# Where the last p*v of each chunk stands, how far apart the score units are, and where the output weights are waited for

## The chip, the cores and the metric

The kernel runs on one core of one Trainium2 chip. The metric is device time in microseconds (us), from the start of the program to its end. The time before is a median of three executions, 561.78 us (561.67 to 562.17). One execution was profiled: 561.61 us, of which the span that the trace covers is 559.9 us.

The engines are named as in the profile: PE is TensorE (PEld its weight loads), DVE is VectorE, ACT is ScalarE, POOL is GpSimd, and SP is SyncE, which issues all DMAs here, in order, from one queue (SPq).

## What is computed

Two branches share the normalized input: windowed causal attention with 32 heads of 18, and a gated feed-forward layer. The result joins them.

```python
xn = layernorm(x)                                  # x is [1, 2048, 576], bfloat16
q, k, v = split(xn @ wqkv)                         # 32 heads, Dh = 18
scores = q @ k.T * Dh ** -0.5                      # a query sees itself and 255 keys before it
p = softmax(where(0 <= i - j < 256, scores, -1e9))
s = (p @ v) @ wo
h = sigmoid(xn @ w_gate) * (xn @ w_up)             # F = 4608
g = silu(h @ w_down)
out = x + s * g
```

## The kernel before

**Tiling.** The 2048 tokens go in four chunks of 512 (`CH`), a chunk in four blocks of 128 tokens. The contracted dimension of 576 is cut into 9 pieces of 64, so that most matmuls use half of PE's rows, and two of them run side by side in the two halves: the profile shows them as `64*128`. A chunk has these stages:

- Layernorm of four blocks, then transposes into `xn` (from chunk 1 on by eight DMA transposes, `xt`, line 250). `xn` is one buffer, so the transposes for the next chunk wait for the last gate/up step of this one.
- q, k and v projections, line 513, `64*128`, and DMA transposes of q and k into `qkp`.
- Gate/up, line 884, `64*128`: 324 *steps* of two matmuls with 512 columns each, 36 tiles of F in all. ACT takes the tanh of a tile, DVE multiplies it into `hT`.
- Attention is laid among the gate/up steps. A *score unit* (line 676, `64*128`) fills two PSUM banks for one group of four heads; ACT takes its exponent into a slot of `expr` (ring of `NEXP` = 10 slots), DVE masks it. A chunk has 8 head groups, with 4 units each in chunk 0 and 5 in the others. After two head groups comes their *p\*v* (line 733, `64*32`, eight small matmuls side by side): 72 matmuls in chunk 0 and 96 in the others. Four p\*v a chunk; `op_pv[c][NHG - 1]` is the fourth. A p\*v releases the `expr` slots of its units.
- After each p\*v a chain on DVE: transpose (line 749), reciprocal, multiplication, transpose back (line 766). Then SP issues copies from `op_` to `oT` (called `oc` in the code): eight behind the last p\*v.
- Output projection `wo` (line 802, `64*128`): two pairs of token blocks, 36 matmuls each.
- Down projection `f2` (line 1009, `128*128`): for each token block 9 steps of four pairs (512 and 64 columns). Chunk 0 runs blocks 0 and 1 step by step in turn, the others one block after the other. The last block of chunk 3 is line 1040.

So PE works with three forms of tile: `64*128` (projections, gate/up, scores, `wo`), `64*32` (p\*v) and `128*128` (down).

**What sets the order.** The program is not written in the order in which it runs. Every operation is an object with dependencies; `schedule()` is a list scheduler that places the operations of all engines on a modelled clock, and `emit()` writes each engine's instructions in that order. `deps` are dependencies that become semaphore waits (or PSUM and buffer hazards); `odeps` only hold the order in the planner and give no wait, since both ends are on PE, which runs in order. An operation of PE that depends on DMAs waits for one semaphore for each of their lanes; waits that the engine has already made are left out.

**What sets it around the change:**

- The k-th score unit of chunk c is not placed ahead of gate/up step `SC_AT[c] + k * SC_STEP[c]` (the list `gated`, in `build_ffn`). `SC_AT` is (108, 0, 0, 0). From chunk 1 on, the first unit is instead put behind the last down step of the chunk before.
- A p\*v of chunks 1 to 3 has an `avoid`: with `PV_AVOID` = (165, 280) and `PACKET` = 256 the planner puts a penalty of 20 us on starting it while the count of PE's instructions, modulo 256, lies from 165 to 280. p\*v has low numbers of columns, so its instructions go by fast.
- The first down step has an order dependency on the last gate/up step (`mms = [prev]`), and each later block on the last p\*v and (from block 2 on) on one `wo` pair.
- The projections of the next chunk run between down blocks 1 and 2. Their order is `QKV_NEXT`; v of block 1 comes behind the first `wo` pair and q of block 2 behind the second, if these have not been placed before.
- `wo` is loaded once, during chunk 0, by 12 DMAs on 12 lanes (`op_wo`, in `build_late_weights`), gated by gate tile 26. In `build`, the first `wo` pass of each pair of chunk 0 depends on all twelve. It also depends on the 16 lanes of the `oc` copies, as every chunk's first pass does.

Of the kernel before, what the change touches and what calls it, by code (L numbers as in the profile page):

```python
# [18 lines left out]
NHG = H // 4  # L19
# [31 lines left out]
SC_PRIO = 1  # L51
KD_PRIO = 0
SC_AT = (108, 0, 0, 0)
SC_STEP = (5.5, 5.0, 5.0, 5.0)
SC_PAD = 200.0
PV_PAD = 350.0
PACKET = 256
# [61 lines left out]
def mm_ns(n):  # L119
    return max(28.0, n / 2.4 + 2.5)  # L120
# [90 lines left out]
class Builder:  # L211
# [98 lines left out]
    def build(self):  # L310
        self.r_xr = Ring(NXR)
        self.r_xnr = Ring(NXNR)
        self.r_xn = Ring(1)
        self.r_w = Ring(RW)
        self.r_t = Ring(RT)
        self.r_pk = Ring(RPK)
        self.r_exp = Ring(NEXP)
        self.r_s = Ring(RS)
        self.r_xf = Ring(RXF)
        self.r_kd = Ring(RKD)  # L320
        self.r_rec = Ring(RREC)
        self.r_bn = Ring(RBN)
        self.op_f1 = {}
        self.build_init()
        self.op_pv = [[None] * NHG for _ in range(NCH)]
        self.op_sc = [[[] for _ in range(NHG)] for _ in range(NCH)]
        self.op_on = [[None] * NHG for _ in range(NCH)]
        self.op_mul = [[None] * NHG for _ in range(NCH)]
        self.all_kd = {}
        self.op_oc = [[[], []] for _ in range(NCH)]  # L330
        self.op_v = [None] * NQB
        self.op_tail = [None] * NHG
        self.op_hT = {}
        self.f2_last = None
        for c in range(NCH):
            self.build_ln(c)
            if c == 0:
                self.build_weights()
                self.build_wd()
            self.build_qkv(c)  # L340
            self.last_mul = None
            self.build_attn(c)
            self.load_x(c)
            self.op_pkz = [self.op("POOL", 2000, lambda e: e.memset(self.pk[:, 1:RPK, :, :], 0.0), f"pkz:{c}",
                                   deps=self.op_on[c], prio=1)]
            if c == 0:
                self.op_wo = []
            self.build_wo(c)
            self.build_ffn(c)
            if c == 0:  # L350
                self.build_late_weights()
                for o in self.ops:
                    if o.name in ("wo:0:00", "wo:0:10"):
                        o.add_dep(self.op_wo)

    def build_init(self):
        op = self.op
# [486 lines left out]
    def build_ffn(self, c):  # L844
# [27 lines left out]
        prev = None  # L872
        gated = [(SC_AT[c] + k * SC_STEP[c], u) for k, u in enumerate(u for l in self.op_sc[c] for u in l)]
        if c > 0:
# [40 lines left out]
        for n0, n1 in zip(cuts, cuts[1:]):  # L915
# [49 lines left out]
            o = self.pe((n1 - n0) * mm_ns(CH), f, f"f:{c}:{low[n0][1]}:{n0}", deps=deps, prio=3, psum=alloc, mode="r64")  # L965
# [19 lines left out]
            prev = o  # L985
            while gated and gated[0][0] <= n0:
                gated.pop(0)[1].odeps.append(o)
        for o in self.op_se:
            o.add_dep(prev)
        mms = [prev]  # L990
        self.r_xn.release(0, prev)
        f2_last = [None] * NWD
        self.f2_ops = f2_ops = {}
        prev = mms
        for blocks in (((0, 1), (2,), (3,)) if c == 0 else ((0,), (1,), (2,), (3,))):
# [5 lines left out]
            for q in range(NWD):  # L1001
                for i in blocks:
                    def f_f2(e, q=q, i=i, ps=banks[i]):
                        b = ps.banks[0] * 512
                        for fl in range(WDG):
                            ft = q * WDG + fl
                            lhsT = self.hT[:, ft, i * P:(i + 1) * P]
                            for n0, n1 in ((0, 512), (512, D)):
# [4 lines left out]
                    o = self.op("PE", WDG * (mm_ns(512) + mm_ns(64)), f_f2, f"f2:{c * QPC + i}:{q}", deps, 3,  # L1013
                                alloc=[banks[i]] if q == 0 else [], mode="full",
                                odeps=prev + ([self.op_wop[i - FIN]] if q == 0 and i >= FIN else [])
                                + ([self.op_pv[c][NHG - 1]] if q == 0 and i > 0 else []))
                    banks[i].users.append(o)
                    prev = [o]
# [326 lines left out]
```

## Time and profile before

| | before |
|---|---|
| median of three executions | 561.78 us |
| the profiled execution | 561.61 us |
| its span | 559.9 us |
| DVE busy | 317.7 us (57%) |
| ACT busy | 274.7 us (49%) |
| DMA share of 16 engines, queue q1 | 61.3% |
| granted TensorE clock in every slice | 1.00 |
| score units, chunk 1 | the first at 156.54 us, the last at 220.41 us |
| p\*v starts, chunk 0 | 59.20, 71.65, 84.53, 95.02 us |
| p\*v starts, chunk 1 | 174.07, 190.63, 206.97, 223.75 us |
| p\*v starts, chunk 2 | 310.70, 326.42, 342.76, 359.54 us |
| p\*v starts, chunk 3 | 448.55, 464.25, 486.42, 503.20 us |
| down starts (blocks 0 and 1), chunks 0 to 3 | 103.25, 245.77, 383.50, 516.93 us |

The last p\*v of a chunk stands 8 to 24 us ahead of the down projection. `wo` runs in chunk 0 among the next chunk's projections (from 125.45 us), in chunk 1 between gate/up and down (from 241.04 us), in chunk 2 inside the last gate/up steps (from 376.40 us) and in chunk 3 between down blocks 1 and 2 (from 534.45 us).

How to read the lines further on: the timeline merges neighbouring instructions of one kind, and a line gives start, duration, engine, source line, operation, output and inputs, shape and count. A matmul's shown duration is that of one instruction from start to modelled end; matmuls overlap, so the pace is read from starts, not from durations. A few matmul records are missing from the trace: the down blocks show 141 of 144.

### The profile page before, as it was taken

How to read it: one execution, taken by the hardware profiler on the slowest of the kernel's cores; microseconds unless marked ns; L12 is line 12 of the kernel's file. 1: busy time of each engine (PE TensorE's matmuls, PEld its weight loads, DVE VectorE, ACT ScalarE, POOL GpSimd, SP SyncE). 2: the span in 40 equal slices, each digit the busy share in tenths (PEclk: the TensorE clock that was granted, in tenths of full speed). 3: DMA queues.
4: the chain of work that ended last, by engine and by line, in shares of the span. 5: the costliest groups of instructions: out<-in, count | busy, mean ns of one | idle time of the engine just before them, and what ended most of it. 6: DMA issues, size and time to landing. Idle time of an engine off the chain costs nothing.

```text
span 559.9 us, 16728 instructions
## 1 busy us (share of the span) xinstructions
PE 552.2 (99%) x7115; PEld 310.3 (55%) x7138; DVE 317.7 (57%) x911; ACT 274.7 (49%) x394; POOL 30.0 (5%) x58
## 2 busy tenths in 40 slices
PE   8999999999999999999999999999999999999997
PEld 5755555458555555455755555545665555554554
DVE  6436999334157989522417899841331788575012
ACT  8436876114076778221408776622131887482021
POOL 3000110100000100100000011010000000001000
PEclk9999999999999999999999999999999999999999
DMA  8999779859945665441993556543399354751010
GB/s 202 222 207 232 171 189 212 233 92 135 184 103 129 133 155 130 105 77 36 157 217 75 130 126 150 118 99 64 59 170 194 76 129 108 170 131 42 1 43 21
DMA packets 125921, 73.22 MB, mean 131 GB/s; under 512 B 54680, under 2 KB 125336, under 8 KB 125848
## 3 DMA queue, kind: packets, MB, share of 16 engines
q1 hardware_dynamic: 125848, 72.16, 61.3%
q8 instruction: 56, 0.92, 0.7%
q14 instruction: 17, 0.14, 0.1%
HBM read 55.48 MB, written 2.36 MB: 103 GB/s over the span
## 4 chain that ended last, share of the span: by engine, by line
PE 97%; DMA 1%; SPq 1%; issue 0%; ACT 0%; DVE 0%; ACTq 0%
PE ps L884 50%; PE ps L1009 23%; PE ps L513 9%; PE ps L676 6%; PE ps L733 4%; PE ps L802 3%; PE ps L1040 2%; DMA wqkv_sb<-in_A_wqkv_dram 1%; SPq L251 1%; DMA qkp<-pk 1%; ACT pk L567 0%; DVE expr L1073 0%; ACT expr L1071 0%; PE ps L487 0%; DVE expr L1075 0%
## 5 line engine op out<-in xcount | busy, mean ns | idle before, releaser
L884 PE MATMUL ps<-xn,wgs 64*128 64x512 bf16 x2522 | 299.7, 376 | 0.0
L884 PEld LDWEIGHTS ps<-xn,wgs 64*128 64x128 bf16 x2522 | 121.8, 94 | 113.6 <-issue 1.4
L691 ACT ACTIVATE expr<-ps 128x1024 bf16<-128x1024 f32 (+1 forms) x152 | 149.6, 1031 | 20.5 <-PE ps L676 20.5
L902 DVE SCALAR_TENSOR_TENSOR hT<-tring,ps 128x512 bf16<-128x512 bf16 x144 | 98.3, 683 | 63.3 <-PE ps L884 36.4
L1009 PE MATMUL ps<-wd_sb,hT 128*128 128x64 bf16 (+1 forms) x1057 | 131.1, 284 | 2.1 <-issue 1.1
L898 ACT ACTIVATE tring<-ps 128x512 bf16<-128x512 f32 x144 | 87.4, 607 | 91.8 <-PE ps L884 70.4
L1009 PEld LDWEIGHTS ps<-wd_sb,hT 128*128 128x128 bf16 x1080 | 68.2, 98 | 65.5 <-issue 2.5
L1071 ACT ACTIVATE expr<-ps 128x576 bf16<-128x576 f32 (+2 forms) x17 | 10.6, 623 | 127.8 <-PE ps L1009 120.2
L705 DVE TENSOR_TENSOR expr<-expr,m 128x256 bf16<-128x256 bf16 (+1 forms) x272 | 60.0, 265 | 4.3 <-ACT expr L691 4.1
L1073 DVE SCALAR_TENSOR_TENSOR expr<-expr,ps 128x576 bf16<-128x576 bf16 (+2 forms) x17 | 12.2, 719 | 84.1 <-ACT expr L1071 84.1
L676 PE MATMUL ps<-qkp,kd 64*128 64x320 bf16 (+4 forms) x720 | 57.1, 252 | 0.0
L513 PE MATMUL ps<-wqkv_sb,xn 64*128 64x288 bf16 x864 | 54.5, 283 | 0.5 <-DMA wqkv_sb<-in_A_wqkv_dram 0.4
L660 DVE TENSOR_SCALAR kd<-qkp,hm 128x256 bf16<-128x256 bf16 x176 | 40.5, 290 | 22.5 <-DMA qkp<-pk 20.8
L676 PEld LDWEIGHTS ps<-qkp,kd 64*128 64x128 bf16 x720 | 34.1, 94 | 34.1 <-issue 2.2
L513 PEld LDWEIGHTS ps<-wqkv_sb,xn 64*128 64x128 bf16 x864 | 44.4, 94 | 9.4 <-issue 1.4
L749 DVE STREAM_TRANSPOSE pk<-ps 128x512 f32<-128x512 f32 x32 | 21.5, 700 | 15.8 <-PE ps L733 15.8
L715 POOL COPY qkp<-qkp 128x256 bf16<-128x256 bf16 x24 | 10.8, 450 | 271.3 <-DVE kd L660 271.3
L766 DVE STREAM_TRANSPOSE op__63<-pk 128x512 bf16<-128x512 bf16 x32 | 22.2, 700 | 0.0
L733 PEld LDWEIGHTS ps<-expr,vau 64*32 64x32 bf16 x1440 | 18.1, 92 | 7.4 <-issue 4.7
L733 PE MATMUL ps<-expr,vau 64*32 64x320 bf16 (+4 forms) x1440 | 20.8, 254 | 0.0
L802 PE MATMUL ps<-wo_sb,oT 64*128 64x288 bf16 x288 | 18.7, 283 | 0.1
L613 DVE CAST vau<-ps 64x288 bf16<-64x288 f32 x32 | 14.6, 457 | 7.2 <-PE ps L513 6.6
(52 smaller groups left out, 192.5 us busy)
## 6 DMA issues: line engine op xcount, KB each, us to landing
wgs<-in_B_w_gate_dram SPq DMA_DIRECT2D x47, 240.0 KB, 3.8
wgs<-in_B_w_up_dram SPq DMA_DIRECT2D x47, 240.0 KB, 4.8
wgs<-in_B_w_up_dram SPq DMA_DIRECT2D x47, 192.0 KB, 4.0
wgs<-in_B_w_gate_dram SPq DMA_DIRECT2D x47, 192.0 KB, 4.6
wd_sb<-in_B_w_down_dram SPq DMA_DIRECT2D x9, 576.0 KB, 7.4
xf<-in_A_x_dram SPq DMA_DIRECT2D x18, 144.0 KB, 2.4
out_dram<-xf SPq DMA_DIRECT2D x15, 144.0 KB, 2.0
xr<-in_A_x_dram SPq DMA_DIRECT2D x14, 144.0 KB, 4.5
```

Source lines behind the costliest of these rows:

```text
L513: r = e.matmul(self.bank(ps, HV, hf), self.xn[r0:r0 + 64, k, i * P:(i + 1) * P], self.wqkv_sb[r0:r0 + 64, j, k, :], start=(k == 0), stop=( ...
L660: return e.tensor_scalar(dst, src, self.hm[:, half:half + 1], None, ALU.mult)
L676: i = e.matmul(self.bank(ps, 512, r)[:, pos * 64:(pos + n) * 64], w, self.qkp[r0:r0 + 64, hg, q0 * 64:(q0 + n) * 64], start=True, stop=Tru ...
L691: return e.activation(self.expr[:, es, :, 0:ncol], src, ACTF.Exp, scale=SM_SCALE)
L705: return e.tensor_tensor(ap, ap, m, ALU.mult)
L733: r = e.matmul(self.bank(ps2[s_])[32 * cg:32 * cg + 32, q0 * 64:(q0 + n) * 64], vf[:, v0:v0 + 32], self.expr[p0:p0 + 64, es, cg % 2, pos * ...
L766: t2 = self.op("DVE", dve_ns(CH), lambda e, on=on: e.transpose(self.op_[:, hg % NOT, :], on.rearrange("p g d -> p (g d)")), f"t2:{c}:{hg}" ...
L802: r = e.matmul(self.bank(ps2[w], HV, n), self.oT[r0:r0 + 64, kt, qi * P:(qi + 1) * P], self.wo_sb[r0:r0 + 64, kt, n * HV:(n + 1) * HV], st ...
L884: return e.matmul(self.bank((pg, pu)[gu][ft]), w, self.xn[r0:r0 + 64, i, :], start=first, stop=last, tile_position=(r0, 0))
L898: return e.activation(self.tring[:, st_, :], self.bank(ps), ACTF.Tanh, scale=0.5)
L902: return e.scalar_tensor_tensor(self.hT[:, ft, :], self.tring[:, st_, :], 1.0, self.bank(ps), ALU.add, ALU.mult)
L1009: r = e.matmul(self.ps[:, b + n0:b + n1], lhsT, self.wd_sb[:, q, fl, n0:n1], start=(ft == 0), stop=(ft == NFT - 1))
```

## The change

Three things, in four places:

- `SC_STEP` becomes 7 instead of 5 for chunks 1 to 3.
- The last p\*v of each chunk gets an order dependency on the last gate/up step, loses its `avoid`, and takes the place of that step as what the first down step comes behind.
- Twelve dependencies are added: down step q of block 1 of chunk 0 waits for some of the loads of `wo`: q = 4 for the loads 0, 5 and 10, q = 5 for 1, 6 and 11, q = 6 for 2 and 7, q = 7 for 3 and 8, q = 8 for 4 and 9. The dependencies of the two `wo` passes on all twelve stay.

```diff
-SC_STEP = (5.5, 5.0, 5.0, 5.0)
+SC_STEP = (5.5, 7.0, 7.0, 7.0)
...
                 for o in self.ops:
                     if o.name in ("wo:0:00", "wo:0:10"):
                         o.add_dep(self.op_wo)
+                for k, o in enumerate(self.op_wo):
+                    self.f2_ops[(1, 4 + k % 5)].add_dep(o)
...
         for o in self.op_se:
             o.add_dep(prev)
-        mms = [prev]
+        last_pv = self.op_pv[c][NHG - 1]
+        last_pv.odeps.append(prev)
+        last_pv.avoid = None
+        mms = [last_pv]
         self.r_xn.release(0, prev)
```

## The prediction

> **What bounds the kernel now.** I read the page first: engines, then the chain that ended last.
>
> ```profile
> span 559.9 us, 16728 instructions
> PE 552.2 (99%) x7115; PEld 310.3 (55%) x7138; DVE 317.7 (57%) x911; ACT 274.7 (49%) x394; POOL 30.0 (5%) x58
> ...
> q8 instruction: 56, 0.92, 0.7%
> ...
> PE 97%; DMA 1%; SPq 1%; issue 0%; ACT 0%; DVE 0%; ACTq 0%
> ```
>
> PE holds 97% of the chain, and no other engine is near. So only two kinds of time can be won: matmuls left out (the change leaves none out), and gaps between them. "Busy 99%" hides gaps, since a matmul's shown end is modelled; I read the gaps from starts in PE's timeline, here around the last p\*v of chunk 1 and the end of its gate/up:
>
> ```profile
> 220.63 3.19 PE L884 MATMUL ps<-xn,wgs 64*128 64x512 bf16 x28
> 223.75 1.38 PE L733 MATMUL ps<-expr,vau 64*32 64x320 bf16 x96
> 225.06 13.77 PE L884 MATMUL ps<-xn,wgs 64*128 64x512 bf16 x126
> ...
> 241.04 4.57 PE L802 MATMUL ps<-wo_sb,oT 64*128 64x288 bf16 x72
> 245.77 17.59 PE L1009 MATMUL ps<-wd_sb,hT 128*128 128x64 bf16 x141 [0.16 <-issue]
> ```
>
> From 225.06 to 241.04 PE runs 148 gate/up matmuls (126 and the 22 in lines left out), 74 pairs: 15.98 / 74 = 0.216 us a pair, or 0.422 ns a column. This is the pace without gaps. Against it:
>
> - into p\*v: 14 pairs from 220.63 should end at 223.65; p\*v starts at 223.75. **0.10 us** for the step from `64*128` to `64*32`.
> - p\*v: 96 matmuls, eight abreast, stream 2560 columns (40 blocks of 64, from the code), 1.08 us at this pace; from 223.75 to 225.06 are 1.31. The 0.23 over holds the step back to `64*128` and what the twelve groups lose inside; I put the step at **0.13**, with 0.23 as its upper bound.
> - into down: 36 pairs of `wo` take 4.42 at 0.1228 us a pair (steady pace of such pairs, below) and should end at 245.46. The first down matmul's record is missing (141 of 144); it has 512 columns, so it began at 245.77 - 0.22 = 245.55. **0.09 us**; in chunk 0 the same sum gives 0.12 (96.00 + 32 x 0.216 = 102.91 against 103.03). I take 0.10.
>
> A third kind of gap, before the first `wo` in chunk 0:
>
> ```profile
> 120.77 4.58 PE L513 MATMUL ps<-wqkv_sb,xn 64*128 64x288 bf16 x72
> 125.45 2.38 PE L802 MATMUL ps<-wo_sb,oT 64*128 64x288 bf16 x36
> 127.66 2.38 PE L513 MATMUL ps<-wqkv_sb,xn 64*128 64x288 bf16 x36
> ```
>
> From 125.45 to 127.66 go 18 pairs: 0.1228 us each. The 36 pairs from 120.77 should thus end at 125.19, and `wo` starts at 125.45: **0.26 us**. Nothing that it reads was late (SP issued the last `wo` load at 101.6 and the last copy to `oT` by 109.0), so I read it as the row of 28 lane waits ahead of the pass.
>
> **The change part by part.**
>
> *Last p\*v ahead of down, four times.* Matmuls: the same number. Steps of form before, a chunk: into p\*v 0.10, out 0.13, into down 0.10. After: into p\*v 0.10, and from `64*32` to `128*128`, which this trace does not show. Bounds by the nearest rows: 0.09 (the cheapest step seen) and 0.23 (the dearest that leaving p\*v can be). I take 0.13, the price of leaving p\*v for gate/up, as what drains is the same. Saved: one step of 0.10 a chunk, **-0.40 us** in four chunks (bounds 0 and -0.56). `wo` of chunks 1 and 2 can no longer stand in front of down; it joins the projections, as in chunk 0, all `64*128`: no step added.
>
> The Trainium skill (TensorEngine Tiling (Array Packing), Key Properties) has it that every change of tiling mode drains TensorE. The three gaps of 0.09 to 0.13 agree; by this rule the step from p\*v into down has a price too, which speaks against a saving above 0.56.
>
> What becomes late: the chain behind p\*v. In chunk 3 p\*v ended at 504.51 and the eight copies were issued from 508.94 to 514.45, 9.9 us after it. Now p\*v ends about 1.4 us after the last gate/up step, and `wo` runs after two down blocks (17.6 us) and, in chunks 1 and 2, four projections (4.4 us). In chunk 3: 9.9 + 3.2 (median landing) = 13.1 of 17.6 us. In chunks 1 and 2 the same copies meet the eight transposes on SP, in front of which they ended before:
>
> ```profile
> 229.49 6.27 SPq L251 DMA_DIRECT2D oT<-op__63  x8
> 235.86 0.82 SPq L251 DMA_DIRECT2D xf<-in_A_x_dram  x2
> 241.24 11.12 SPq L250 DMA_TRANSPOSE xn<-xnr  x8
> ```
>
> If the copies come last: 241.24 + 11.12 + 6.27 = 258.6, landed by 261.8; `wo` is due at 241.04 + 0.10 + 1.31 + 0.13 + 17.6 + 4.4 = 264.6. If the transposes come last they land at 261.2 (median 2.6) for a third block whose projection starts 11 us into the stage. **0**, hidden by the down blocks. In chunk 0 SP was already busy from 102.55 to 120.0 with the same 16 transfers, only in the other order. The last projections' evictions, the memset on POOL (1.8 us) and the final steps of blocks 0 and 1 that wait for `wo` go as they went in chunk 0, where PE had no gap but the 0.26.
>
> *Score units every 7 steps.* Same units. Two small gaps of the trace are units that came too early in a chunk (162.39 + 5 x 0.216 = 163.47 against 163.58, and 0.10 at 434.38). Wider spacing takes one or both away: **-0.10** (bounds 0 and -0.21).
>
> *Waits for `wo` spread.* The first pass keeps 16 lanes of copies, as in chunk 2, where `wo` at 376.40 followed gate/up without a gap (360.85 + 72 x 0.216 = 376.40): **-0.26** (bounds 0 and -0.26). Behind the waits on PE stand the down steps themselves. A step takes 0.98 us and gets two or three more waits; the last `wo` load was issued at 101.6 and the slowest landed 9.7 us later, 111.3; step 4 of block 1 comes at 104.4 + 9 x 0.98 = 113.2. **0**, at worst 0.26. In chunks 1 and 2 the 16 waits now follow projections, whose instructions go by faster than gate/up's: 0 taken, at worst 16/28 of 0.26 = 0.15 each.
>
> Sum: -0.40 - 0.10 - 0.26 = **-0.76 us**: span 559.1, and 560.85 for the profiled execution (561.61, itself 0.17 under the median). Against the median of 561.78: **561.0**. With all terms at their ends: 560.7 to 562.3.
>
> 0.2% of this kernel, 1.12 us, is what a measurement can tell from no change; the forecast lies within it.
>
> **Rivals.**
>
> 1. *More is saved.* If the way out of p\*v hides in the change to down altogether, a chunk saves 0.23, and with all gaps gone 0.92 + 0.26 + 0.21 = 1.39: **560.4**. For it: these gaps are all that stands between PE and its pace. Against: no step between forms in this trace is free. 0.16.
> 2. *Slower: the last scores come too late.* p\*v must now follow the last gate/up step, and down must follow p\*v. Gates end at step 39 x 7 = 273 of 324. Before they ended at 195, yet the last unit of chunk 1 ran 88 steps from the end, at 236: 41 steps late; in chunk 3 at 254, 59 late. p\*v needs its exponents and masks: 3.3 us from the last unit (220.41 to 223.75), 15 steps. It decides once a unit is over 36 steps late. Were the lag carried over, chunk 1 is 5 steps late (1.1 us) and chunk 3 has 23 steps (5 us) uncovered, less 0.76: **567**. Against: p\*v to p\*v takes 16.5 us before, and ten units at 7 steps take 15.1 + 2.2 + 1.4 = 18.7; the lag came from gates faster than this cycle and shouldn't build up. 0.06, part of it with a single chunk hit (562.1).
> 3. *Slower: instruction blocks.* PE's instructions come in 56 blocks (q8), 0.92 MB, about 255 each. 0.7% of 16 engines' 559.9 us over 56 is 1.12 us a block. The last p\*v now lies anywhere in a block. If three of them wait for one whole block: 3.36 - 0.76, **564.4**. It decides if a block runs out sooner than the next arrives: 192 instructions in 1.31 us and 64 of gate/up in 3.5, 4.8 us against 1.12, and in chunk 0, which was never shifted, p\*v shows no gap. 0.06. The Trainium skill (Runtime: NRT & Kernel Launch, Instruction fetch mechanics) says that crossing a block of 256 is mostly hidden; by it this rival is worth nothing.
> 4. *Slower: copies late.* If landing takes over 6.0 us (264.6 - 258.6) in chunks 1 and 2; the slowest copy of this trace took 9.3. One chunk at 9.3 is 3.3 - 0.76: **564.3**. Against: the slow landings fall in stretches with weight loads, of which none run there. 0.06.
>
> The order itself can't fail to be made: p\*v and its neighbours are all on PE, which runs in order.
>
> **Chances.** Forecast 0.66 (own range 560.7 to 562.3), rivals 0.16, 0.06, 0.06, 0.06. Faster 0.16, same 0.66, slower 0.18. The range runs from 560.4, where rival 1 ends, to 563.0, which takes in the ends of the small terms and the milder forms of rivals 2 to 4; their full forms stay outside.
>
> **What would show it.** One p\*v between line 884 and line 1009 in each chunk, followed by a start 0.13 us late; `wo` of chunks 1 and 2 among line 513; the 0.26 us ahead of the first `wo` gone; the last unit of chunks 1 to 3 well ahead of the end of gate/up; no PE gap behind down blocks 0 and 1. It is wrong if p\*v waits for ACT or DVE at the end of gate/up, if the first `wo` waits for copies, or if a gap over 0.3 us stands inside or behind the last p\*v.

## The result, and the profile after

| | before | after |
|---|---|---|
| median, runs side by side | 561.99 us (561.29 to 562.82, 21 runs) | 561.03 us (560.84 to 561.71, 21 runs) |
| the profiled execution | 561.61 us | 561.03 us |
| its span | 559.9 us | 559.3 us |
| first p\*v to last split down block, on PE (first weight loads) | 59.20 to 547.77: 488.57 us | 59.19 to 546.78: 487.59 us |

The ratio of the times is 0.9985, with a 95% interval of 0.998 to 0.9991: faster by 0.15%, surely not slower, and inside the 0.2% that the prediction had called "same"; 21 runs of each tell more than it had allowed. The forecast was 561.0.

The page of the kernel after: span, busy time of the engines, the queue of instruction blocks, and the shares of the chain that ended last.

```profile
span 559.3 us, 16753 instructions
PE 553.2 (99%) x7138; PEld 307.5 (55%) x7138; DVE 320.4 (57%) x911; ACT 279.9 (50%) x394; POOL 29.9 (5%) x58
...
q8 instruction: 56, 0.92, 0.7%
...
PE 98%; SPq 1%; DMA 1%; DVE 0%; issue 0%; ACT 0%
```

The page can't show where under 1 us went (PE's busy time even rises, since 23 matmul records are missing before). PE's timeline can; here chunk 0 and chunk 1 of the kernel after (start, duration of the merged group, engine, line, operation, tiles, form, count):

```profile
99.67 2.32 PE L886 MATMUL ps<-xn,wgs 64*128 64x512 bf16 x19
101.91 1.05 PE L735 MATMUL ps<-expr,vau 64*32 64x320 bf16 x72
102.90 17.82 PE L1014 MATMUL ps<-wd_sb,hT 128*128 128x512 bf16 x144
120.64 4.58 PE L515 MATMUL ps<-wqkv_sb,xn 64*128 64x288 bf16 x72
125.06 2.37 PE L804 MATMUL ps<-wo_sb,oT 64*128 64x288 bf16 x36
127.27 2.37 PE L515 MATMUL ps<-wqkv_sb,xn 64*128 64x288 bf16 x36
...
236.94 2.32 PE L886 MATMUL ps<-xn,wgs 64*128 64x512 bf16 x19
239.19 1.38 PE L735 MATMUL ps<-expr,vau 64*32 64x320 bf16 x96
240.50 17.82 PE L1014 MATMUL ps<-wd_sb,hT 128*128 128x512 bf16 x144
258.25 4.58 PE L515 MATMUL ps<-wqkv_sb,xn 64*128 64x288 bf16 x72
262.67 2.37 PE L804 MATMUL ps<-wo_sb,oT 64*128 64x288 bf16 x36
```

Each chunk now ends its gate/up (L886) with the last p\*v (L735), and down (L1014) follows, with nothing between. The 72 projections from 120.64 take their 36 x 0.1228 = 4.42 us, and `wo` starts at 125.06, on time: the gap of 0.26 is gone. The same sum holds at 258.25 to 262.67, where `wo` of chunk 1 now stands.

Followed from start to start, PE gains 0.11 us at the switch of chunk 0, 0.28 at the first `wo`, 0.23 in chunk 1 (0.12 at the switch, 0.11 from the gap at 163.5 that is gone), 0.13 in chunk 2 and 0.23 in chunk 3 (0.13, and the gap of 0.10 at 434.3 that is gone): 0.98 us together. The last split block shows the sum, first the kernel before, then after:

```profile
547.80 8.98 PE L1040 MATMUL ps<-wd_sb,hT 128*128 128x448 bf16 x72
```

```profile
546.81 8.98 PE L1045 MATMUL ps<-wd_sb,hT 128*128 128x448 bf16 x72
```

That is 0.99 us earlier, and the two medians differ by 0.96. The two profiled executions differ by only 0.58: the last output lands 0.99 us earlier (558.44 for 559.44), but SP's two closing instructions, a branch and a drain, stand 0.49 us apart after and 0.16 before. So below, each kernel is also judged by its *PE stretch*, from the first weight load of the first p\*v to that of the last split down block, which has no program start or end in it. It is read from one profiled execution of each kernel.

### The profile page after: what moved, and what is told of

Same layout as the page of the kernel before. It is cut to its first block, busy times and chain, and to the rows that moved or that the text cites. A ratio compares the mean times of both kernels' runs of the same rounds, so it can differ in the third digit from the quotient of the medians.

```text
span 559.3 us, 16753 instructions
## 1 busy us (share of the span) xinstructions
PE 553.2 (99%) x7138; PEld 307.5 (55%) x7138; DVE 320.4 (57%) x911; ACT 279.9 (50%) x394; POOL 29.9 (5%) x58
## 4 chain that ended last, share of the span: by engine, by line
PE 98%; SPq 1%; DMA 1%; DVE 0%; issue 0%; ACT 0%
PE ps L886 50%; PE ps L1014 24%; PE ps L515 9%; PE ps L678 6%; PE ps L735 4%; PE ps L804 3%; PE ps L1045 2%; SPq L251 1%; DMA wqkv_sb<-in_A_wqkv_dram 1%; DVE expr L1078 0%; ACT expr L1076 0%; PE ps L489 0%; DVE expr L1080 0%; DVE xf L1082 0%
## 5 line engine op out<-in xcount | busy, mean ns | idle before, releaser
L886 PE MATMUL ps<-xn,wgs 64*128 64x512 bf16 x2522 | 298.2, 376 | 0.0
L886 PEld LDWEIGHTS ps<-xn,wgs 64*128 64x128 bf16 x2522 | 121.0, 94 | 116.3 <-issue 1.2
L1014 PE MATMUL ps<-wd_sb,hT 128*128 128x512 bf16 (+1 forms) x1080 | 133.7, 287 | 0.0
L1014 PEld LDWEIGHTS ps<-wd_sb,hT 128*128 128x128 bf16 x1080 | 68.2, 98 | 64.2 <-issue 0.9
L707 DVE TENSOR_TENSOR expr<-expr,m 128x256 bf16<-128x256 bf16 (+1 forms) x272 | 60.7, 267 | 5.4 <-ACT expr L693 5.3
L662 DVE TENSOR_SCALAR kd<-qkp,hm 128x256 bf16<-128x256 bf16 x176 | 40.7, 292 | 12.1 <-DMA qkp<-pk 10.5
L751 DVE STREAM_TRANSPOSE pk<-ps 128x512 f32<-128x512 f32 x32 | 21.1, 696 | 12.2 <-PE ps L735 12.2
L735 PEld LDWEIGHTS ps<-expr,vau 64*32 64x32 bf16 x1440 | 18.0, 92 | 7.4 <-issue 5.9
L735 PE MATMUL ps<-expr,vau 64*32 64x320 bf16 (+4 forms) x1440 | 20.8, 254 | 0.0
```

The source lines that it names most:

```text
L662: return e.tensor_scalar(dst, src, self.hm[:, half:half + 1], None, ALU.mult)
L707: return e.tensor_tensor(ap, ap, m, ALU.mult)
L735: r = e.matmul(self.bank(ps2[s_])[32 * cg:32 * cg + 32, q0 * 64:(q0 + n) * 64], vf[:, v0:v0 + 32], self.expr[p0:p0 + 64, es, cg % 2, pos * ...
L886: return e.matmul(self.bank((pg, pu)[gu][ft]), w, self.xn[r0:r0 + 64, i, :], start=first, stop=last, tile_position=(r0, 0))
L1014: r = e.matmul(self.ps[:, b + n0:b + n1], lhsT, self.wd_sb[:, q, fl, n0:n1], start=(ft == 0), stop=(ft == NFT - 1))
```

## The experiments

### One part alone

Three kernels, each with one part of the change. First the move of p\*v (this edit and the next are shown against the kernel after):

```diff
-SC_STEP = (5.5, 7.0, 7.0, 7.0)
+SC_STEP = (5.5, 5.0, 5.0, 5.0)
...
-                for k, o in enumerate(self.op_wo):
-                    self.f2_ops[(1, 4 + k % 5)].add_dep(o)
```

> Only the last p*v is moved; score units stay at 5 steps and the waits for the output weights stay in one row. Read by the start of the last split down block on PE (547.80 us before, 546.81 after the whole change). Theory (one step of form saved a chunk): 0.49 us of the 0.99 come from here, so it starts at 547.3; the 0.26 us gap ahead of the first output projection and the two gaps of 0.1 us stay. Rival (the move is free and the gain is the waits and the spacing): 547.8. Second rival (with scores bunched at 5 steps the late copies make the output projection of chunks 1 to 3 wait): later than 548.

Measured: 561.29 us against 562.20 before, ratio 0.9989 (0.998 to 0.9998); the PE stretch is 488.11, 0.46 shorter. The four switches give 0.11 to 0.12 us each, 0.45 together. Two other differences cancel. The gaps at score units, expected to stay, lose 0.16 (the one at 163.5 is down to 0.05, the one at 434 is gone). The row of waits is still there, and costs 0.16 more than before:

```profile
120.62 4.58 PE L513 MATMUL ps<-wqkv_sb,xn 64*128 64x288 bf16 x72
125.46 2.38 PE L802 MATMUL ps<-wo_sb,oT 64*128 64x288 bf16 x36 [0.26 <-issue]
```

The projections start 0.15 us earlier than before, `wo` at the same time. Its gap is 125.46 - 120.62 - 4.42 = 0.42, not 0.27. PE's record of semaphore instructions says why (start in us, instruction; a few of the fifteen, which wait for two semaphores each but the first; `$S[101]` and `$S[100]` count DVE's and ACT's instructions, the others are lanes of DMAs):

```
124.670  EVENT_SEMAPHORE  $S[144]>= $S[172]>=
124.776  EVENT_SEMAPHORE  $S[145]>= $S[171]>=
125.036  EVENT_SEMAPHORE  $S[146]>= $S[170]>=
125.142  EVENT_SEMAPHORE  $S[147]>= $S[135]>=
125.248  EVENT_SEMAPHORE  $S[101]>= $S[134]>=
125.354  EVENT_SEMAPHORE  $S[100]>= $S[133]>=
125.430  LDWEIGHTS  wo
```

Every lane had been ready since 114.8 us, yet each instruction takes 0.106 us, and one took 0.26. Before, the row ran without that pause from 123.86 to 125.35; after, it has nine instructions, from 123.74 to 124.75 (with one such pause), and the first weights of `wo` load at 124.94, early enough. That the pause is the crossing into the next block of instructions is a guess: in these two kernels, and in the two further on that spread the waits without the spacing, a block's packet follows 0.7 to 1.3 us later.

The waits alone:

```diff
-SC_STEP = (5.5, 7.0, 7.0, 7.0)
+SC_STEP = (5.5, 5.0, 5.0, 5.0)
...
-        last_pv = self.op_pv[c][NHG - 1]
-        last_pv.odeps.append(prev)
-        last_pv.avoid = None
-        mms = [last_pv]
+        mms = [prev]
```

> Only the twelve waits for the output weights are spread over down steps. Theory (the 0.26 us ahead of the first output projection is the row of lane waits): the gap is gone, the last split down block starts at 547.5, nothing else moves. Rival (the gap is a late copy into oT, which shares the same pass): the gap stays, 547.8. Second rival (the waits only change place): gaps of together 0.26 us inside the down steps of block 1, 547.8.

Measured: 561.88 us, ratio 0.9999 (0.999 to 1.0007); PE stretch 488.43, 0.14 shorter. The gap ahead of `wo` is gone here too (36 pairs from 121.09, `wo` at 125.51). But a new one stands in chunk 2:

```profile
295.94 0.81 PE L886 MATMUL ps<-xn,wgs 64*128 64x512 bf16 x6
296.84 0.40 PE L678 MATMUL ps<-qkp,kd 64*128 64x320 bf16 x6
```

Three pairs from 295.94 end at 296.59; the score unit starts at 296.84, 0.25 late. PE's wait there ends at 296.74, 0.04 us behind a DVE instruction (a multiplication on the down result of the chunk before, line 1075 here). The two gaps of the kernel before end in the same way, 0.04 us behind DVE instructions that end at 163.44 (the scaling into `kd`, line 660) and at 434.23 (line 1073, the same multiplication). The gap near 163.5 stayed here, the one at 434 went, though the spacing is 5 as before.

The spacing alone, 7 in place of 5 (shown against the kernel before):

```diff
-SC_STEP = (5.5, 5.0, 5.0, 5.0)
+SC_STEP = (5.5, 7.0, 7.0, 7.0)
```

> Only the spacing of the score units is 7 instead of 5 in chunks 1 to 3; the last p*v stays inside gate/up, later than before. Theory (two units came 0.1 us too early for their buffers): the gaps at 163.5 and 434.3 us are gone, the last split down block starts at 547.6. Rival (spacing is worth nothing by itself): 547.8. Second rival: the output projection of chunks 1 and 2, now among the next projections with its 16 lane waits behind small matmuls, gains gaps of up to 0.15 us each: 547.9.

Measured: 562.13 us, ratio 1.0002 (0.9993 to 1.0011); PE stretch 488.30, 0.27 shorter. Both gaps at score units are gone, and the time doesn't show it.

### The whole change without the spacing

With the move alone, units every 5 steps left only one gap at a score unit, of 0.05 us. So the other two parts were run together:

```diff
-SC_STEP = (5.5, 7.0, 7.0, 7.0)
+SC_STEP = (5.5, 5.0, 5.0, 5.0)
```

> The whole change but for the spacing: score units stay at 5 steps. Theory (the step of form and the row of waits are the gain; the small gaps ahead of score units come and go from one execution to the next): as the whole change within 0.2 us, 561.0 to 561.3 us, and from the first p*v to the last split down block 487.6 to 487.9 us on PE. Rival (the spacing carries 0.2 us of it): 488.0 or more, with gaps ahead of score units.

Measured: 560.91 us (560.52 to 561.47), ratio 0.998 (0.9972 to 0.9989), PE stretch 487.70. It is the best median of all, not to be told from the whole change (0.998 to 0.9991). The stretch is 0.11 longer, and a gap of 0.05 is left at 163.1. So the spacing is worth nothing that the times could show; on PE it is worth 0.11 us beside the other two parts, and 0.27 alone. Part of the reason may be the end of the program: SP's branch and drain stand 0.16 to 0.17 us apart in the profiles of the kernel before, the move alone, the waits alone, these two together and the restriction turned round further on, and 0.49 to 0.50 in all others, which have units every 7 steps or more in chunk 1. No run was made to find out why.

### What the step from p\*v into down costs

One down step of chunks 1 to 3 is put ahead of the last p\*v. That adds one change of form a chunk and nothing else:

```diff
-        last_pv.odeps.append(prev)
...
-        mms = [last_pv]
+        if c == 0:
+            last_pv.odeps.append(prev)
+        mms = [last_pv if c == 0 else prev]
...
+                    if c > 0 and (i, q) == (0, 0):
+                        last_pv.odeps.append(o)
+                        prev = [last_pv]
```

> The whole change, but in chunks 1 to 3 the last p*v stands one step later, behind the first down step instead of ahead of it: one more step of form, everything else alike. Theory (each change of tile form costs about 0.1 us, wherever it is): the last split down block starts 0.3 us later than with the whole change, at 547.1, and the step from 128*128 into p*v costs 0.09 to 0.10 us. Rival (what was gained is a quiet place for p*v, not a step of form): 546.8.

```profile
236.91 2.32 PE L886 MATMUL ps<-xn,wgs 64*128 64x512 bf16 x19
239.38 0.93 PE L1015 MATMUL ps<-wd_sb,hT 128*128 128x64 bf16 x7 [0.16 <-issue]
240.24 1.38 PE L735 MATMUL ps<-expr,vau 64*32 64x320 bf16 x96
241.78 1.39 PE L1015 MATMUL ps<-wd_sb,hT 128*128 128x64 bf16 x10 [0.16 <-issue]
```

Three changes where the kernel after has two. Measured: 561.62 us, ratio 0.9987 (0.9978 to 0.9996); PE stretch 487.91, 0.32 over the whole change, for 0.3 expected. By the columns streamed, each step between two forms costs 0.09 to 0.13 us; from `64*32` into `128*128` it is 0.10 to 0.11 in the kernel after and 0.12 here, where the first down matmul's record is missing. The Trainium skill (TensorEngine Tiling (Array Packing), Key Properties) says that switching the mode drains TensorE; the trace agrees for every pair of forms here, and no direction is free.

### How far the scores may be spread

With 8.2 steps between units the last of 40 is due behind step 319 of 324:

```diff
-SC_STEP = (5.5, 7.0, 7.0, 7.0)
+SC_STEP = (5.5, 8.2, 8.2, 8.2)
```

> The whole change with score units every 8.2 steps in chunks 1 to 3: the last gate is step 319.8 of 324. Theory (the last p*v needs its exponents and masks, 3.3 us or 15 steps from the last unit, and down must wait for p*v): about 11 steps of 0.216 us are uncovered in each of three chunks, PE stands still for 2.4 to 3.3 us ahead of the last p*v, 7 to 10 us in all: 568 to 571 us. Rival (p*v and down are far enough from the last unit, the wait is covered): 561.0.

Measured: 569.59 us against 562.00, ratio 1.013 (1.0107 to 1.0153); PE stretch 496.96, 9.37 over the whole change. PE's timeline at the end of chunk 1:

```profile
237.52 2.11 PE L886 MATMUL ps<-xn,wgs 64*128 64x512 bf16 x18
239.46 0.38 PE L678 MATMUL ps<-qkp,kd 64*128 64x320 bf16 x4
241.85 1.41 PE L735 MATMUL ps<-expr,vau 64*32 64x320 bf16 x96 [2.00 <-DVE expr L707]
243.59 4.74 PE L1014 MATMUL ps<-wd_sb,hT 128*128 128x64 bf16 x26 [0.33 <-issue]
```

Now the last unit stands behind gate/up and p\*v waits for its mask (L707, DVE): 239.68 to 241.85, 2.17 us, and the same in chunks 2 and 3: 6.5 of the 9.37. That is less than the 2.4 to 3.3 expected of each; the time fell into the forecast range only with the rest, which comes after the wait. Windows of the same kernel (stretch, its length, PE busy and instructions, granted clock, DMA share, GB/s):

```profile
242.40:243.00 0.60, 0.60 (x77) 1.00 0.71 158
243.00:243.50 0.50, 0.25 (x31) 0.51 0.15 33
243.50:244.50 1.00, 0.91 (x4) 0.50 2.02 130
...
245.50:246.00 0.50, 0.50 (x4) 0.50 0.75 178
246.00:246.50 0.50, 0.50 (x5) 0.58 0.40 85
```

The clock falls to 0.50 at 243.0, when PE has been at work again for over 1 us, and is back at about 246.4. Chunk 3 shows the same from 522.9 to about 526.3, chunk 2 doesn't. Twice 3.4 us at half pace cost at most 2 x 1.7 = 3.4 us; 2.9 are left of the 9.37. The four executions order themselves in the same way: 567.12 us at a mean granted clock of 0.999, 569.08 at 0.997, 570.11 and 570.93 (the profiled one) at 0.994. The Trainium skill (TensorE: Matmul & The Clock Gate, Part 1) gives some 3.4 us for an idle window that lowers the clock and as much work to raise it. The 3.4 us of low clock agree; an idle time of 2.2 us was enough here in two cases of three. In the trace's record of the clock the two falls lie 279.9 us apart, 82 steps of 3.413 us. Counted in such steps, all of the idle time of chunks 1 and 3 lies in the step that ends with the fall, but in chunk 2 the step ends 0.16 us before PE goes on. That the idle share of a step decides would fit these three cases (2.2, 2.2 and 2.0 us); no run tested it.

With 7.7 steps:

```diff
-SC_STEP = (5.5, 7.0, 7.0, 7.0)
+SC_STEP = (5.5, 7.7, 7.7, 7.7)
```

> The whole change with score units every 7.7 steps in chunks 1 to 3: the last gate is step 300, 24 steps ahead of the end. Theory (15 steps cover the exponents and masks): nothing is uncovered, 561.0 us. Rival (units lag behind their gates as they did at 5 steps, by 32 to 59 steps): p*v waits, 562 to 570 us.

Measured: 561.38 us, ratio 0.9988 (0.9979 to 0.9996), PE stretch 487.77, 0.18 over the whole change: one gap of 0.155 at 461.33, where a score unit waits for DVE's transpose (L751), and no p\*v waits. The cliff lies between 7.7 and 8.2.

### What the instruction blocks cost

The change exempts the last p\*v from the planner's `avoid`. Here all p\*v are exempt:

```diff
-        o.avoid = PV_AVOID if c > 0 else None
+        o.avoid = None
```

> The whole change, and no p*v keeps its restriction on the count of instructions, so that four of the nine other p*v of chunks 1 to 3 stand elsewhere in their instruction blocks. Theory (a block lasts 4.8 us even around a p*v and arrives in 1.1): nothing, 546.8 for the start of the last split down block and 561.0 us. Rival (a p*v in the restricted place waits for its instructions): 0.3 to 1.1 us for each p*v that falls there, 561.5 to 564.

Measured: 562.34 us (561.73 to 565.02), ratio 1.0013 (1.0002 to 1.0023). That is slower than the whole change, whose interval ends at 0.9991, and PE's stretch is 487.93. The same restriction turned round, so that the first three p\*v of chunks 1 to 3 start where the planner had kept them from:

```diff
-                    if o.avoid and (at - o.avoid[0]) % PACKET < o.avoid[1] - o.avoid[0]:
+                    if o.avoid and (at - o.avoid[0]) % PACKET >= o.avoid[1] - o.avoid[0]:
```

> The whole change, with the restriction turned round for the first three p*v of chunks 1 to 3: they may start only where before they might not, at a count of 165 to 280 modulo 256. Theory (instruction blocks always arrive in time): no gap inside or behind them, 546.8 and 561.0 us. Rival (that place makes PE wait for instructions): nine p*v at 0.3 to 1.1 us, 564 to 571 us.

Measured: 561.17 us, ratio 0.9989 (0.998 to 0.9998), PE stretch 488.02. Of nine p\*v so placed one leaves a gap, of 0.35 us behind the p\*v of 331.65:

```profile
334.92 0.81 PE L886 MATMUL ps<-xn,wgs 64*128 64x512 bf16 x6
335.92 1.04 PE L886 MATMUL ps<-xn,wgs 64*128 64x512 bf16 x8 [0.19 <-issue]
```

The kernel without `avoid` was then run again, for another profile:

> The kernel of e6 once more, because its median lay 1.3 us above that of the whole change while its profile shows only 0.3 us more. Theory (its loss is real and comes from some p*v that now stand where instructions run out): again 562 us or more, and a profile of a slower execution shows a gap with no wait in or behind a p*v. Rival (that run was disturbed): 561.0 to 561.3, as with the whole change.

Measured: 562.19 us (561.55 to 565.86), ratio 1.001 (0.9997 to 1.0023), PE stretch 488.75, 1.16 over the whole change. Its timeline in chunk 2:

```profile
331.92 1.38 PE L735 MATMUL ps<-expr,vau 64*32 64x320 bf16 x96
333.45 1.67 PE L886 MATMUL ps<-xn,wgs 64*128 64x512 bf16 x14
334.96 0.38 PE L678 MATMUL ps<-qkp,kd 64*128 64x320 bf16 x6
335.18 0.60 PE L886 MATMUL ps<-xn,wgs 64*128 64x512 bf16 x4
336.55 0.39 PE L678 MATMUL ps<-qkp,kd 64*128 64x256 bf16 x4 [0.78 <-issue]
```

Two pairs from 335.18 and PE has nothing until 336.55, 0.94 us, and waits for no engine ("issue"). The packet of an instruction block starts at 333.89 in this profile, at 333.23 in the one of the turned restriction and at 333.02 in the first without it; PE goes on at 336.55, 335.92 and 335.73: 2.66, 2.69 and 2.71 us after it. So PE had run out of instructions, and the three times follow the packet. Windows of the same kernel, over that p\*v and behind it (columns as above):

```profile
331.00:333.00 2.00, 1.97 (x96) 1.00 0.97 230
333.00:335.40 2.40, 2.40 (x67) 1.00 1.08 221
```

All 16 DMA engines are busy with other loads. Around the last p\*v of the kernel after they are less so (chunks 2, 1 and 3; a share of 0.00, 0.74 and 0.02):

```profile
374.50:377.50 3.00, 3.00 (x70) 1.00 0.00 0
239.20:242.50 3.30, 3.30 (x115) 1.00 0.74 52
514.40:518.00 3.60, 3.60 (x117) 1.00 0.02 5
```

That full queues delay the block is argued from these rows, not shown: no run took the loads away. In these three profiles it is always the second p\*v of chunk 2; why only this one starves stays open, and so does why the kernel without `avoid` reaches 565 us in the slowest execution of each run (565.02 and 565.86, at a mean granted clock of 0.997; neither has a profile), when the one with the restriction turned round stays below 561.8.

### `wo` of chunk 3 inside gate/up

To save the two changes of form around `wo` in chunk 3 (down, `wo`, down), its `wo` is put among the last gate/up steps there, which puts the last p\*v back among them too:

```diff
-SC_STEP = (5.5, 7.0, 7.0, 7.0)
+SC_STEP = (5.5, 7.0, 7.0, 5.0)
...
-        last_pv.odeps.append(prev)
...
+        if c < NCH - 1:
+            last_pv.odeps.append(prev)
+        else:
+            mms = [prev] + self.op_wop
+            self.op_pv[c][5].avoid = None
```

> The whole change, but in chunk 3 score units stay at 5 steps, the last two p*v are free of the restriction on the count, the last one stays inside gate/up, and the output projection goes between the last gate/up steps, so that it no longer stands alone between two down blocks. Theory (only changes of tile form count): two of 0.096 us less at the output projection, one of 0.10 us more at p*v: 0.1 us earlier than the whole change, 487.5 us from the first p*v to the last split down block. Rival (copies to oT are not there yet when the output projection stands ahead of down): PE waits there, by up to 3 us.

Measured: 561.18 us, ratio 0.9987 (0.9979 to 0.9996), PE stretch 487.75: 0.16 over the whole change where 0.10 under it was expected. The copies were in time. Some of the missing 0.26 stands behind the p\*v of 479.67, which here has no `avoid`:

```profile
482.95 2.35 PE L886 MATMUL ps<-xn,wgs 64*128 64x512 bf16 x18
484.70 0.10 PEld L886 LDWEIGHTS ps<-xn,wgs 64*128 64x128 bf16 x2 [0.36 <-issue]
484.94 0.47 PE L678 MATMUL ps<-qkp,kd 64*128 64x256 bf16 x3
485.24 0.27 PE L678 MATMUL ps<-qkp,kd 64*128 64x256 bf16 x1
```

The weight loads stop for 0.36 us and go on at 484.70, 2.75 us after a block's packet (481.95), as above. Then a unit of four score matmuls shows as three and one: the two halves of PE no longer run in step, up to the next p\*v. How much of the 0.26 that is can't be read off, so the version stays unproven.

## Why the prediction was right, and where it was off

- **Bound.** PE alone, as said: every gain was a gap on PE, and the medians moved by what PE's starts moved (0.96 and 0.99).
- **One step of form saved per chunk, -0.40.** The mechanism holds. Measured 0.11 to 0.13 a chunk, 0.48 in all, and 0.45 in the experiment with the move alone. The saving is the step into down that falls away, taken at 0.10, so it was mis-sized by 0.01 to 0.03 a chunk. The 0.13 for leaving p\*v was too high as well (0.10 to 0.11 by the columns; the row that it came from also held losses inside p\*v), but it stands on both sides of the sum and drops out. That both ways out cost the same was right: from its start to the start of what follows, p\*v takes 1.31 us ahead of gate/up (223.75 to 225.06 before) and ahead of down (239.19 to 240.50 after).
- **Waits spread, -0.26.** Right in place and size: 0.28 after, and the gap is gone in the experiment with the waits alone, too. That the gap is the row of waits was a reading then; the row of 0.106 us an instruction shows it. It holds 27 lanes, not 28, and the counters of DVE and ACT. The 16 waits left in chunks 1 and 2, bounded at 0.15, left no gap: nine instructions fit into what PE has queued.
- **Spacing, -0.10.** Both gaps went, -0.21, the far bound, and the cause given for it holds for one of them. The gap near 163.5 stands in all four profiles that have units every 5 steps in chunk 1 (0.11, 0.05, 0.11 and 0.05 us) and in none with 7. The gap at 434 stands in the kernel before alone: it also went with units every 5 steps, and one of 0.25 us came at 296.84. Whether a unit comes too early depends on when DVE is done as well as on the spacing, and no median shows the difference.
- **Sum.** -0.76 was forecast and -0.98 measured on PE: 0.08 more at the four switches, 0.11 at the second small gap, 0.02 at the waits. The time of 561.0 was met to 0.03 us partly by luck: it was set against a median of 561.78, which was 561.99 beside the kernel after. The times settle only the whole: the medians of the parts move by 0.91, 0.32 and 0.07 us with intervals of about 0.5 to each side, where their stretches move by 0.46, 0.14 and 0.27.
- **Rival 1, more is saved.** Half true by size, false by reason: leaving p\*v for down isn't free, as the same 1.31 us shows.
- **Rival 2, last scores too late.** It doesn't come true at 7 steps: the last units run at 230.68, 366.34 and 503.95 us, 8.5 to 10.5 us ahead of p\*v. In chunk 1 the last unit is 13 steps behind its gate, not 41: the lag wasn't carried over. The rival decides between 7.7 and 8.2, and there it costs more than its price of waiting, by the clock.
- **Rival 3, instruction blocks.** It doesn't come true for this change: the last p\*v of the three chunks show no gap, though the one of chunk 2 starts at a count of 214 of 256 in PE's instruction records, inside the range that `avoid` keeps off. But the prediction's argument against it, 4.8 us for a block against 1.12 for its packet, was too weak: what counts is about 2.7 us from the packet's start, and how late the packet starts. The Trainium skill (Runtime: NRT & Kernel Launch, Instruction fetch mechanics) calls the crossing mostly hidden; here it left gaps of 0.11 to 0.94 us, always behind p\*v in the middle of gate/up, where the DMA engines were full (a share of 0.96 to 1.01 over the p\*v).
- **Rival 4, copies late.** No: `wo` follows the projections without a gap in chunks 1 and 2 (258.25 + 4.42 = 262.67), and in chunk 3 the down blocks (533.46).

## What to carry to other kernels

On a kernel bound by one engine at 99%, look for gaps between starts, and count changes of matmul form: here each costs some 0.1 us, so a stage in another form is best put where the form changes anyway. Long rows of waits, even for what has long been ready, are not free on the engine's queue: spread them over slow instructions. A stage moved to the end of its producer needs its inputs done well ahead, since after two of three waits of 2.2 us some 1.4 us each were lost to the lower clock.

## What the runs showed that was not expected

- A PE semaphore instruction takes 0.106 to 0.111 us for one or two semaphores, all satisfied; fifteen in a row outlast what PE has queued by 0.27 us, nine don't.
- After an idle time of 2.2 us on PE the granted clock was 0.50 for 3.4 us in two of three cases, starting 1.2 and 0.1 us after work had resumed.
- PE can run out of instructions behind a burst of short matmuls: it went on 2.66 to 2.75 us after the start of the block's packet in all four profiles that show it.
- In one run the two halves of PE stayed out of step for 12 us after such a stall, up to the next p\*v.
